# Stores of split weight tiles move from the sync engine's queue to GpSimd's

## The chip, the cores and the metric

The kernel runs on one core of a Trainium2 chip. The metric is the device time of one execution in microseconds (us). A core has a matrix engine (PE, with its weight loads PEld), a vector engine (DVE), a scalar engine (ACT), GpSimd (POOL) and a sync engine (SP). Each works through its own list of instructions in order; they wait for one another by semaphores. Transfers between device memory (HBM) and on-chip memory run on DMA engines and are started by an instruction in one engine's list, called here the issue. A transfer has landed when its semaphore says so.

## The reference

Causal attention over 4 x 12 heads of 448 x 64, then two feed-forward blocks over the 1792 x 768 tokens:

```python
x = softmax(mask(q @ k.T / 8)) @ v          # 4 x 12 heads, then joined to 1792 x 768
a = x @ w1;  b = x @ w2                     # 768 -> 1024
y = ((a * b) @ w3) @ w_out                  # 1024 -> 1024 -> 768
h = y @ w_in                                # 768 -> 2048
out = (h - np.tanh(h)) @ w_out2             # 2048 -> 768
```

All inputs are fp32, and the answer is wanted to fp32 accuracy.

## The kernel before

Every matrix product is made of three products of split numbers: each fp32 operand becomes a high part and a low part, and `gemms` (L411 to L413) adds high x low, low x high and high x high into one PSUM tile. The two weights w3 and w_out are multiplied with each other first (`product`). The tokens are worked in two halves of 896, each in two blocks of 384 and 512 columns.

Weights are split once, by `convert`. For each weight tile (a `Job`) the raw bits are loaded (`load`, L295, ring `raw` of two buffers), rescaled on ACT (`low`, L304), put together on DVE (`rounded`, L314, L317 and L321, ring `t` of two buffers), rounded to the high part (`high`, the copy of L267) and subtracted to give the low part (`rest`, the subtraction of L270 on POOL or DVE). The first half of the tokens uses some of these tiles on the spot. The split tiles are also stored to HBM (`store`, L327), because both halves need them, and read back later by `fetch` (L375). The 56 stored tiles are 16 of w1 and w2 (buffers `hl`, ring of three, to `sc12`), 16 of w_in (4 through the single buffer `cvi`, 12 through the two buffers `cvo`, to `sci`) and 24 of the last w_out (through the same two buffers `cvo`, to `sco`). A `cvo` tile is used by nothing else: its buffer is free for the next job but one when its store has landed.

The split of the last 24 tiles runs beside the products of the second half of the tokens: `bilinear` makes a and b, with two PSUM buffers (`r_mm`, L252). The tile of a is copied out by ACT or DVE (`keep`, L267), the tile of b is multiplied with it by DVE (`mult`, L801), and the product is split into the `g` tiles (L267 on ACT, then L270 on POOL). After it `project` runs with eight PSUM buffers.

The order of each engine's list is fixed when the program is built. The class `Plan` keeps a model clock for each engine and for the DMA queue and writes down the step that can start first. `store` asks the model for DMA time alone (`yield dma(...)`), and no time of the engine that issues it. So its instruction goes into the issuing engine's list at the place that the model clock of the DMA queue gives.

Of the kernel before, what the change touches and what calls it, by code (L numbers as in the profile page):

```python
# [19 lines left out]
F32 = mybir.dt.float32  # L20
# [177 lines left out]
def act(n, psum=False):  # L198
    return "ACT", (0.104 if psum else 0.147) + n / 1400
# [8 lines left out]
def dves(n):  # L208

    return "DVE", 0.068 + n / 960, True  # L210


def dve2(n):

    return "DVE", 0.068 + n / 1920, True


def pool(n):
    return "POOL", 0.00244 * n, True
# [11 lines left out]
def dma(size):  # L231
    return "DMA", max(0.5, size / 330e3)
# [3 lines left out]
def body(ctx: ExitStack, tc: tile.TileContext, qkd, vd, vd4, w12, w3t, wo, w_in, wo2, out):  # L236
    nc = tc.nc
    V, A, G, SP, PE = nc.vector, nc.scalar, nc.gpsimd, nc.sync, nc.tensor
# [27 lines left out]
    def copy(eng, out, in_):  # L266
        A.copy(out=out, in_=in_) if eng == "ACT" else V.tensor_copy(out=out, in_=in_)  # L267

    def sub(eng, out, in0, in1):
        (V if eng == "DVE" else G).tensor_tensor(out=out, in0=in0, in1=in1, op=ALU.subtract)  # L270
# [17 lines left out]
    def convert(jobs, r_raw, r_t):  # L288

        def load():  # L290
            for j in jobs:
                plan.rank(j.rank)
                j.raw = yield r_raw
                yield dma(P * j.n * 8)
                SP.dma_start(out=j.raw.t[:, :j.n].rearrange("p n t -> p (n t)"), in_=j.src.bitcast(U32))  # L295
                plan.set(j.loaded)

        def low():
            for j in jobs:
                plan.rank(j.rank)  # L300
                yield j.loaded
                u = j.raw.t[:, :j.n, 0]
                yield act(j.n + 130)
                A.activation(out=u, in_=u, func=AF.Copy, scale=2.0 ** -29)  # L304
                plan.set(j.low)

        def rounded():
            for j in jobs:
                plan.rank(j.rank)
                yield j.loaded  # L310
                j.t = yield r_t
                raw, t, n = j.raw.t, j.t.t[:, :j.n], j.n
                yield dve2(1.25 * n)
                V.tensor_scalar(out=t, in0=raw[:, :n, 1], scalar1=3, scalar2=0x3FFFFFF8,  # L314
                                op0=ALU.logical_shift_left, op1=ALU.bitwise_and)
                yield dves(n)
                V.scalar_tensor_tensor(out=t, in0=raw[:, :n, 1], scalar=0xC0000000, in1=t,  # L317
                                       op0=ALU.bitwise_and, op1=ALU.bitwise_or)
                yield j.low
                yield dves(1.1 * n)  # L320
                V.tensor_tensor(out=t, in0=t, in1=raw[:, :n, 0], op=ALU.add)  # L321
                plan.done(j.raw)
                plan.set(j.rounded)

        def store(j):
            yield dma(P * j.n * 8)
            SP.dma_start(out=j.scratch, in_=j.buf.t[:, :, :j.n].bitcast(F32))  # L327
            plan.done(j.buf)
            plan.set(j.stored)

        def high():
            for j in jobs:
                plan.rank(j.rank)
                yield j.rounded
                j.parts = yield from j.dest(j)
                copy((yield [act(j.n), dve2(j.n)]), j.parts[0], j.t.t[:, :j.n].bitcast(F32))
                plan.set(j.high)

        def rest():
            for j in jobs:  # L340
                plan.rank(j.rank)
                yield j.high
                hi, lo = j.parts
                sub((yield [pool(j.n), dves(j.n)]), lo, j.t.t[:, :j.n].bitcast(F32), hi.bitcast(F32))
                plan.done(j.t)
                if j.scratch is not None:
                    j.buf.users = 1 + j.used
                    plan.spawn(store(j), j.rank)
                plan.set(j.ready)

        for f in (load, low, rounded, high, rest):
            plan.spawn(f(), jobs[0].rank)
# [761 lines left out]
```

## Time and profile before

| what | us |
|---|---|
| median of 3 runs (lowest 1064.9, highest 1068.66) | 1067.23 |
| the profiled execution | 1062.6 |
| its span, first to last instruction | 1060.8 |
| PE busy in the span | 1036.4 |
| DVE busy | 643.3 |
| ACT busy | 619.4 |
| POOL busy | 242.5 |

The span is the profiled execution without the 1.8 us around it. A busy time is the sum over an engine's instructions; issuing a DMA or waiting is not counted as busy. An average over the span hides that stages differ; the stretch between 460 and 580 us is the one that the rows below look at most.

### The profile page before, as it was taken

Reading aid. Unit: us, or ns where it says so; the run is one execution under the profiler, and the core shown is the slowest. Engines: PE = TensorE matmul, PEld = TensorE weight load, DVE = VectorE, ACT = ScalarE, POOL = GpSimd, SP = SyncE. Lnnn points to the kernel's source line nnn. Section 1 sums busy time; section 2 is a strip of 40 time slices with the busy share of each in tenths; the row PEclk is TensorE's granted clock in tenths of the full one; section 3 lists DMA queues with packets and bytes.
Section 4 is the critical chain, followed back from the end, with each engine's and each line's share of the span. In section 5 each row is a group of like instructions: output and inputs, shape, how many; then the busy total and the mean of one; then the engine's idle time right before and its main releaser. Section 6 shows DMA issues by size and latency. Waiting matters only on the chain.

```text
span 1060.8 us, 19813 instructions
## 1 busy us (share of the span) xinstructions
PE 1036.4 (98%) x7680; PEld 899.3 (85%) x7680; DVE 643.3 (61%) x1316; ACT 619.4 (58%) x1353; POOL 242.5 (23%) x188
## 2 busy tenths in 40 slices
PE   5799999999999999999999999999999999999998
PEld 3577788778888989888998989899888988988987
DVE  7886556667665466656565377384756655474742
ACT  6997868788776243433432488573736556553620
POOL 3542131222223400124532022121111111121210
PEclk8999999999999999999999999999999999999999
DMA  7674449877764798999998333233333543233124
GB/s 265 205 215 161 121 149 315 298 255 253 251 223 159 295 366 301 347 323 319 354 326 300 142 118 119 90 129 109 109 110 117 167 140 115 92 120 117 44 87 155
DMA packets 72318, 209.03 MB, mean 197 GB/s; under 512 B 6113, under 2 KB 21473, under 8 KB 70689
## 3 DMA queue, kind: packets, MB, share of 16 engines
q1 hardware_dynamic: 72224, 207.77, 57.0%
q8 instruction: 60, 0.98, 0.4%
q14 instruction: 34, 0.27, 0.1%
HBM read 155.45 MB, written 52.30 MB: 196 GB/s over the span
## 4 chain that ended last, share of the span: by engine, by line
PE 91%; ACT 3%; DMA 2%; DVE 2%; issue 1%; POOL 0%; SPq 0%; ACTq 0%; DVEq 0%
PE mm L411 28%; PE mm L413 27%; PE mm L412 27%; PE pv L683 3%; PE sc L657 2%; PE att L541 1%; DMA raw<-w3t 1%; ACT p L501 1%; PE att L488 1%; PE att L513 1%; ACT pt L267 1%; ACT raw L304 1%; DVE p L459 1%; DMA qk<-qkd 1%; DVE t L321 0%
## 5 line engine op out<-in xcount | busy, mean ns | idle before, releaser
L411 PE MATMUL mm<-x,hl 128*128 128x384 f32 (+1 forms) x768 | 282.1, 367 | 0.0
L413 PE MATMUL mm<-x,hl 128*128 128x384 f32 (+1 forms) x768 | 278.8, 363 | 0.0
L412 PE MATMUL mm<-x,hl 128*128 128x384 f32 (+1 forms) x768 | 278.6, 363 | 0.0
L270 POOL TENSOR_TENSOR g<-g 128x384 fp32r<-128x384 f32 (+1 forms) x64 | 76.7, 1199 | 371.1 <-ACT g L267 371.1
L411 PEld LDWEIGHTS mm<-x,hl 128*128 128x128 f32 x768 | 144.1, 188 | 18.7 <-issue 2.0
L413 PEld LDWEIGHTS mm<-x,hl 128*128 128x128 f32 x768 | 144.1, 188 | 15.3
L412 PEld LDWEIGHTS mm<-x,hl 128*128 128x128 f32 x768 | 144.2, 188 | 14.7
L413 PE MATMUL mm<-g,w 128*128 128x384 f32 (+1 forms) x384 | 139.6, 364 | 0.0
L412 PE MATMUL mm<-g,w 128*128 128x384 f32 (+1 forms) x384 | 139.4, 363 | 0.0
L411 PE MATMUL mm<-g,w 128*128 128x384 f32 (+1 forms) x384 | 139.1, 362 | 0.0
L897 DVE SCALAR_TENSOR_TENSOR g<-r,g 128x512 f32<-128x512 f32 (+1 forms) x192 | 124.7, 659 | 20.4 <-ACT r L888 17.6
L888 ACT ACTIVATE r<-sq,cst 128x384 f32<-128x384 f32 (+1 forms) x192 | 123.6, 666 | 8.0 <-DVE g L897 8.0
L411 PE MATMUL mm<-g,hl 128*128 128x384 f32 (+1 forms) x320 | 116.3, 363 | 2.1 <-POOL g L270 2.1
L413 PE MATMUL mm<-g,hl 128*128 128x384 f32 (+1 forms) x320 | 113.0, 353 | 0.0
L412 PE MATMUL mm<-g,hl 128*128 128x384 f32 (+1 forms) x320 | 112.9, 353 | 0.0
L881 DVE SCALAR_TENSOR_TENSOR g<-sq,mm 128x384 f32<-128x384 f32 (+1 forms) x64 | 39.6, 619 | 109.2 <-ACT th L879 108.6
L314 DVE TENSOR_SCALAR t<-raw 128x512 uint32<-128x512 uint32 (+1 forms) x80 | 52.3, 654 | 69.6 <-DMA raw<-wo 39.1
L875 ACT ACTIVATE sq<-mm 128x384 f32<-128x384 f32 (+1 forms) x64 | 34.7, 543 | 92.5 <-PE mm L413 92.4
L304 ACT ACTIVATE raw<-raw 128x512 uint32<-128x512 uint32 (+1 forms) x80 | 63.9, 799 | 33.7 <-DMA raw<-wo 16.3
L270 POOL TENSOR_TENSOR hl<-t,hl 128x512 fp32r<-128x512 f32 (+1 forms) x32 | 52.1, 1635 | 134.0 <-ACT hl L267 99.1
L321 DVE CUSTOM_DVE_ANT_0 t<-raw,t 128x1024 uint16<-128x1024 uint16 (+1 forms) x80 | 75.1, 938 | 6.7 <-ACT raw L304 0.2
L412 PEld LDWEIGHTS mm<-g,w 128*128 128x128 f32 x384 | 72.1, 188 | 8.0
(81 smaller groups left out, 1599.0 us busy)
## 6 DMA issues: line engine op xcount, KB each, us to landing
hl<-sci SPq DMA_DIRECT2D x32, 768.0 KB, 4.6
w<-sco SPq DMA_DIRECT2D x48, 512.0 KB, 3.5
raw<-w SPq DMA_DIRECT2D x16, 768.0 KB, 5.7
sc<-hl SPq DMA_DIRECT2D x16, 768.0 KB, 4.4
raw<-w_in SPq DMA_DIRECT2D x16, 768.0 KB, 6.7
hl<-scp SPq DMA_DIRECT2D x12, 1024.0 KB, 6.5
hl<-sc SPq DMA_DIRECT2D x16, 768.0 KB, 7.0
raw<-wo SPq DMA_DIRECT2D x24, 512.0 KB, 6.7
```

What stands on the lines that cost most here:

```text
L270: (V if eng == "DVE" else G).tensor_tensor(out=out, in0=in0, in1=in1, op=ALU.subtract)
L304: A.activation(out=u, in_=u, func=AF.Copy, scale=2.0 ** -29)
L314: V.tensor_scalar(out=t, in0=raw[:, :n, 1], scalar1=3, scalar2=0x3FFFFFF8, op0=ALU.logical_shift_left, op1=ALU.bitwise_and)
L321: V.tensor_tensor(out=t, in0=t, in1=raw[:, :n, 0], op=ALU.add)
L411: PE.matmul(ps, wh, xl, start=k == 0, stop=False)
L412: PE.matmul(ps, wl, xh, start=False, stop=False)
L413: PE.matmul(ps, wh, xh, start=False, stop=k == last)
L683: PE.matmul(ps.t[e * D:(e + 1) * D, a, have[0] * 32:P], v.t[r, kb, e], x, start=kb == 0, stop=kb == block(a, 4 - 1))
L875: A.activation(out=sq, in_=h, func=AF.Square)
L881: V.scalar_tensor_tensor(out=g, in0=sq, scalar=LEAD, in1=h, op0=ALU.mult, op1=ALU.mult)
L888: A.activation(out=rk.t[:, :n], in_=sq, func=AF.Square, bias=cst[:, k:k + 1])
L897: V.scalar_tensor_tensor(out=g, in0=rk.t[:, :n], scalar=QUAD[k][1], in1=g, op0=ALU.add, op1=ALU.mult)
```

## The change

The store of a split tile is issued by GpSimd instead of the sync engine:

```diff
         def store(j):
             yield dma(P * j.n * 8)
-            SP.dma_start(out=j.scratch, in_=j.buf.t[:, :, :j.n].bitcast(F32))
+            G.dma_start(out=j.scratch, in_=j.buf.t[:, :, :j.n].bitcast(F32))
             plan.done(j.buf)
             plan.set(j.stored)
```

The planner's model is the same, so the lists of PE, DVE and ACT are the same row for row. The 56 stores leave SP's list and stand in POOL's, each at the place that the model clock gave it.

POOL's list at the first tiles of the last w_out, before. `cvo_5471`, `cvo_5536`, `cvo_5576` and `cvo_5628` are the buffers of tiles 0 to 3, `g` the split of the product a * b; a name such as DMAHW4 is the semaphore of a transfer that was started by SP, DMASW0 of one started by POOL.

```order
L270 TENSOR_TENSOR g_5150<-asb_5442,g_5150 128x512 [waits Activation_49]
L270 TENSOR_TENSOR cvo_5471<-t_5436,cvo_5471 128x512 [waits DMAHW4_49,DMAHW5_49,DMAHW3_49,DMAHW7_49,DMAHW1_49,Activation_49]
L270 TENSOR_TENSOR g_5150<-asb_5411,g_5150 128x384 [waits Activation_49]
L270 TENSOR_TENSOR cvo_5536<-t_5485,cvo_5536 128x512 [waits DMAHW4_49,DMAHW1_49,DMAHW6_49,DMAHW0_49,Activation_49]
L270 TENSOR_TENSOR cvo_5576<-t_5542,cvo_5576 128x512 [waits DMAHW4_49,Activation_49]
L270 TENSOR_TENSOR g_5150<-asb_5557,g_5150 128x512 [waits Activation_49]
L270 TENSOR_TENSOR g_5150<-asb_5525,g_5150 128x384 [waits Activation_49]
L270 TENSOR_TENSOR cvo_5628<-t_5582,cvo_5628 128x512 [waits DMAHW7_49,Activation_49]
```

The same place in POOL's list now:

```order
L270 TENSOR_TENSOR g_5150<-asb_5442,g_5150 128x512 [waits Activation_49]
L327 DMA sci_15_123<-cvo_5430 128x1536 [waits DMASW7_49]
L270 TENSOR_TENSOR cvo_5471<-t_5436,cvo_5471 128x512 [waits DMASW4_49,DMASW2_49,DMASW6_49,DMASW0_49,Activation_49]
L270 TENSOR_TENSOR g_5150<-asb_5411,g_5150 128x384 [waits Activation_49]
L270 TENSOR_TENSOR cvo_5536<-t_5485,cvo_5536 128x512 [waits DMASW5_49,DMASW3_49,DMASW7_49,DMASW1_49,Activation_49]
L327 DMA sco_0_124<-cvo_5471 256x1x512 [waits Pool_49]
L270 TENSOR_TENSOR cvo_5576<-t_5542,cvo_5576 128x512 [waits DMASW0_49,Activation_49]
L327 DMA sco_1_125<-cvo_5536 256x1x512 [waits Pool_49]
L270 TENSOR_TENSOR g_5150<-asb_5557,g_5150 128x512 [waits Activation_49]
L270 TENSOR_TENSOR g_5150<-asb_5525,g_5150 128x384 [waits Activation_49]
L327 DMA sco_2_126<-cvo_5576 256x1x512 [waits Pool_49]
L270 TENSOR_TENSOR cvo_5628<-t_5582,cvo_5628 128x512 [waits DMASW1_49,Activation_49]
```

The store of tile 0 stands behind the subtraction of tile 1, that of tile 1 behind the subtraction of tile 2, that of tile 2 behind two subtractions of `g`.

POOL's list at tiles 9 to 14 now (`cvo_5854`, `cvo_5908`, `cvo_5942`, `cvo_5977`, `cvo_6025`, `cvo_6068`):

```order
L327 DMA sco_9_133<-cvo_5854 256x1x512 [waits Pool_49]
L270 TENSOR_TENSOR cvo_5908<-t_5853,cvo_5908 128x512 [waits DMASW0_49,Activation_49]
L270 TENSOR_TENSOR cvo_5942<-t_5907,cvo_5942 128x512 [waits DMASW1_49,Activation_49]
L327 DMA sco_10_134<-cvo_5908 256x1x512 [waits Pool_49]
L270 TENSOR_TENSOR g_5151<-asb_5926,g_5151 128x512 [waits Activation_49]
L327 DMA sco_11_135<-cvo_5942 256x1x512 [waits Pool_49]
L270 TENSOR_TENSOR cvo_5977<-t_5941,cvo_5977 128x512 [waits DMASW2_49,Activation_49]
L270 TENSOR_TENSOR g_5151<-asb_5894,g_5151 128x384 [waits Activation_49]
L270 TENSOR_TENSOR cvo_6025<-t_5976,cvo_6025 128x512 [waits DMASW3_49,Activation_49]
L327 DMA sco_12_136<-cvo_5977 256x1x512 [waits Pool_49]
L270 TENSOR_TENSOR cvo_6068<-t_6031,cvo_6068 128x512 [waits DMASW4_49,Activation_49]
```

Before, the subtractions stand there in the same order and nothing between them; the stores of tiles 10 and 12 now stand behind the subtraction of the next tile.

SP's list at the first of these tiles, before:

```order
L327 DMA sci_15_123<-cvo_5430 128x1536
L375 DMA hl_5496<-sc12_8_94 128x2x768
L295 DMA raw_5484<-wo2 128x1024
L327 DMA sco_0_124<-cvo_5471 256x1x512
L375 DMA hl_5555<-sc12_9_95 128x2x768
L295 DMA raw_5541<-wo2 128x1024
L327 DMA sco_1_125<-cvo_5536 256x1x512
L295 DMA raw_5581<-wo2 128x1024
```

And now:

```order
L375 DMA hl_5496<-sc12_8_94 128x2x768
L295 DMA raw_5484<-wo2 128x1024
L375 DMA hl_5555<-sc12_9_95 128x2x768
L295 DMA raw_5541<-wo2 128x1024
L295 DMA raw_5581<-wo2 128x1024
```

SP keeps its loads and fetches in their order, and no longer waits for POOL's subtraction between them.

## Rows read from the trace of the kernel before

**Rows 1.** The page: busy time (share of span) and count; the chain's shares by engine.
```profile
PE 1036.4 (98%) x7680; PEld 899.3 (85%) x7680; DVE 643.3 (61%) x1316; ACT 619.4 (58%) x1353; POOL 242.5 (23%) x188
...
PE 91%; ACT 3%; DMA 2%; DVE 2%; issue 1%; POOL 0%; SPq 0%; ACTq 0%; DVEq 0%
```

**Rows 2.** Stretches: length, then busy us and count by engine, clock, DMA share, GB/s.
```profile
466.00:536.00 70.00, 70.00 (x348) 62.53 (x347) 42.40 (x54) 28.91 (x50) 33.21 (x25) 1.00 0.95 334
...
700.00:800.00 100.00, 100.00 (x501) 90.27 (x500) 60.44 (x101) 49.22 (x91) 17.12 (x14) 1.00 0.34 111
```

**Rows 3.** Waits of PE, 160 to 600 us: total us, times, longest.
```profile
PE pv L683 <- issue: 1.0, 2, 0.7
```

**Rows 4.** Waits of ACT and DVE from 460 to 580 us, in the same columns.
```profile
DVE t L314 <- DMA raw<-wo: 38.3, 18, 4.8
...
ACT cvo L267 <- DMA sco<-cvo: 15.3, 6, 5.4
```

**Rows 5.** Waits of SP's queue over the whole span, in the same columns.
```profile
SPq L327 <- POOL cvo L270: 39.7, 21, 3.3
```

**Rows 6.** DMA issues: count, KB of one, median us from issue to landing.
```profile
w<-sco SPq DMA_DIRECT2D x48, 512.0 KB, 3.5
...
sc<-hl SPq DMA_DIRECT2D x16, 768.0 KB, 4.4
...
sco<-cvo SPq DMA_DIRECT2D x24, 512.0 KB, 5.4
...
sci<-cvo SPq DMA_DIRECT2D x12, 768.0 KB, 8.0
...
sci<-cvi SPq DMA_DIRECT2D x4, 768.0 KB, 3.2
```

**Rows 7.** POOL by time: start us, length us, instruction, [idle before, what ended it].
```profile
434.51 3.57 POOL L270 TENSOR_TENSOR g<-asb,g 128x512 fp32r<-128x512 f32 x2 [68.01 <-ACT g L267]
...
463.96 1.29 POOL L270 TENSOR_TENSOR g<-asb,g 128x512 fp32r<-128x512 f32 x1 [12.43 <-ACT g L267]
466.94 1.30 POOL L270 TENSOR_TENSOR cvo<-t,cvo 128x512 fp32r<-128x512 f32 x1 [1.69 <-DMA sci<-cvo]
...
471.51 1.29 POOL L270 TENSOR_TENSOR cvo<-t,cvo 128x512 fp32r<-128x512 f32 x1 [2.11 <-ACT cvo L267]
...
511.08 1.21 POOL L270 TENSOR_TENSOR g<-asb,g 128x384 fp32r<-128x384 f32 x1
...
533.29 1.33 POOL L270 TENSOR_TENSOR cvo<-t,cvo 128x512 fp32r<-128x512 f32 x1 [3.85 <-ACT cvo L267]
...
575.75 1.29 POOL L270 TENSOR_TENSOR cvo<-t,cvo 128x512 fp32r<-128x512 f32 x1 [3.01 <-ACT cvo L267]
```

**Rows 8.** SP's queue by time, in the same columns: two stores.
```profile
460.77 0.33 SPq L327 DMA_DIRECT2D sci<-cvo  x1
...
472.83 0.55 SPq L327 DMA_DIRECT2D sco<-cvo  x1
```

**Rows 9.** ACT by time, in the same columns.
```profile
466.24 0.62 ACT L267 CAST cvo<-t 128x512 fp32r<-128x512 f32 x1 [2.36 <-DMA sci<-cvo]
...
470.81 0.62 ACT L267 CAST cvo<-t 128x512 fp32r<-128x512 f32 x1 [2.50 <-DVE t L321]
471.34 0.58 ACT L267 COPY asb<-mm 128x512 f32<-128x512 f32 x1
```

**Rows 10.** DVE by time, in the same columns.
```profile
467.21 1.32 DVE L314 TENSOR_SCALAR t<-raw 128x512 uint32<-128x512 uint32 x1 [2.95 <-DMA raw<-wo]
...
479.37 0.43 DVE L314 TENSOR_SCALAR t<-raw 128x512 uint32<-128x512 uint32 x1 [3.66 <-DMA raw<-wo]
...
480.44 0.55 DVE L801 TENSOR_TENSOR asb<-mm,asb 128x384 f32<-128x384 f32 x1
```

**Rows 11.** PE by time, in the same columns: the first matmul of a tile.
```profile
481.09 0.45 PE L411 MATMUL mm<-x,hl 128*128 128x512 f32 x1
```

## The prediction

> **What bounds the kernel now.** I read the page first. PE is busy for 98% of the span and makes up 91% of the chain that ended last [rows 1], so a change counts only where it makes PE wait or spares it a wait. Next the stretches: from 466 to 536 us, where many of the moved stores lie, PE is busy for 70.00 of 70.00 us and runs 348 matmuls, 4.97 in a us; from 700 to 800 us, where no tile is split or stored, it runs 501, or 5.01 in a us [rows 2]. So the stage with the stores runs as fast as the stage without them. The list of waits says the same: between 160 and 600 us, which holds all 56 stores, PE waited for 1.0 us in all, and for nothing that the trace names [rows 3]. There is nothing here for the change to win back. What there is to lose is told by the engines that empty PE's two PSUM buffers. DVE's multiplication at 480.44 ends at 480.99, and PE starts the next tile in that buffer at 481.09 [rows 10, 11]: DVE had 0.1 us to spare. DVE and ACT are that late because in their fixed lists they first wait for the splitting of the weights: DVE 38.3 us for raw tiles, ACT 15.3 us, six times, for a stored `cvo` buffer to come free [rows 4]. So the question is whether the moved stores make those waits longer.
>
> **What the change removes.** SP loses 56 issues, and with them its wait for POOL's subtraction, 39.7 us in 21 waits [rows 5]; those 21 stores left in the moment in which they were ready. The loads behind them may go out sooner. Worth: at most the 1.0 us that PE waits, and I take 0.
>
> **What it adds on POOL.** 56 issues. What one costs on POOL the trace of before doesn't show. SP takes 0.33 to 0.55 us for one [rows 8]; a POOL subtraction of 512 columns takes 1.29 us [rows 7]. I take SP's 0.55, which is already part of the landing times below, since nothing is computed; 1.29 would add 0.74 to each. As work it fits: POOL is busy 33.21 of 70 us [rows 2], and the 15 stores there would add 8 to 20. A price below nothing is excluded: the instruction is new on POOL.
>
> **What it moves, where it costs nothing.** The 16 `hl` stores land 4.4 us after their issue [rows 6]. Their ring has three buffers, and a tile stays in its buffer anyway until PE has used it for two blocks of 18 matmuls, 2 x 18 x 0.20 = 7.2 us (0.20 is 70/348). That hides the store; without this cover it would cost one landing at each turn of the ring. The four `cvi` stores land in 3.2 us [rows 6]; on POOL they follow their own subtraction directly, as on SP, so only a dearer issue could cost, 4 x 0.74 = 3 us at most. Of the 12 `sci` stores from `cvo` the first seven find POOL empty: it had waited 68.01 us when it began the subtraction at 434.51 [rows 7]. They leave when their tile is ready, as before.
>
> **What it moves, where it costs.** From 434 us on POOL's list holds the splits of the product, and stores stand behind them. The last `sci` store left SP at 460.77 [rows 8]; on POOL it stands behind the subtraction of 463.96, which ends at 465.25 [rows 7]. With the median landing of 8.0 [rows 6] it is through at 473.25. Tile 1 of the last w_out needs that buffer, and its copy on ACT began at 470.81 [rows 9]: 2.4 us late.
>
> Then the 24 `sco` stores. There are two buffers, so tile n+2 can be rounded only when the store of tile n has landed. Before, a store left as soon as its own subtraction had ended: that of tile 1 ends at 472.80 and SP issues at 472.83 [rows 7, 8]. Now the lists show the store of tile 0 behind the subtraction of tile 1, that of 1 behind 2, 4 behind 5, 7 behind 8, 10 behind 11 and 12 behind 13. Where store n waits for subtraction n+1, and subtraction n+2 for the landing of store n, the two buffers no longer overlap: one follows the other. One such link costs a landing of 5.4 us [rows 6] plus the copy on ACT and the subtraction, from 466.24 to 468.24, 2.0 us [rows 7, 9]: 7.4 us. The longest path from subtraction 1 to subtraction 14 goes through the tiles 1, 2, 3, 5, 6, 8, 9, 11, 12, 13, 14. Nine of its steps are such links (3 to 5, 6 to 8 and 9 to 11 are the ordinary loop over two tiles, with one subtraction of `g`, 1.21 us [rows 7], ahead of store 9); 12 to 13 is a plain step at the mean distance, 61.8/13 = 4.75. That makes 9 x 7.4 + 1.2 + 4.75 = 72.6 us. Before, subtraction 1 ends at 472.80 and subtraction 14 at 534.62 [rows 7], 61.8 us. So the splitting falls 10.8 us behind, with the 2.4 from above 13.2.
>
> **What of it reaches PE.** ACT and DVE are bound to the order of their lists, so a late `cvo` copy holds up the copy out of PSUM right behind it (470.81, then 471.34 [rows 9]). With two PSUM buffers an evacuation can be late by at most one tile, 18 x 0.20 = 3.6 us, less its own 0.58; at 480.44 nothing is left of that. I take half of 3.0 as spare: 13.2 - 1.5 = 11.7, about 12 us that PE waits.
>
> From tile 14 on (until 577.04, the end of the last subtraction [rows 7]) the same links cost again: six of them and two plain steps, 6 x 7.4 + 2 x 4.75 = 53.9 us instead of 42.4. But by then `project` runs with eight PSUM buffers, six more than before, each a tile of 24 matmuls: 6 x 24 x 0.20 = 29 us of cover. I cost it at nothing; without the cover it is 11.5 us more.
>
> Sum: the profiled execution took 1062.6 us, its span 1060.8; with 12 us the span becomes 1073 and the execution 1075. The median of the runs, 1067.2, lies 4.6 above the profiled execution, so I forecast 1067.2 + 12 = **1079 us**.
>
> The bounds are those of the landing. The lowest is 3.5 us, the fetch of the same 512 KB at a time when little else is moved, the highest 8.0, the `sci` stores in the crowded stretch [rows 6]. A link is then 5.5 or 10.0. I take 5.4 since it is the same transfer at the same place, with the DMA engines 95% busy [rows 2].
>
> The Trainium skill (DMA: Bandwidth & Descriptors, section Latency and other measured facts) gives about 1 us to the first byte for a transfer started by GpSimd and about 0.6 for one started by SP. By it each link would be 0.4 longer and the time about 1083; no run so far shows it.
>
> **Rivals.**
>
> *No change, 1067.* A store of 768 KB lands in 3.2 us where little else is queued and in 8.0 behind SP's loads [rows 6]. In a queue of its own it may no longer stand behind them. At 3.5 us the path is 9 x 5.5 + 6 = 55.5, under 61.8, and the last `sci` store is through at 465.25 + 3.5 = 468.8, ahead of 470.81: nothing is late. It decides from a landing of 4.2, a link of 6.2. Against it: the DMA engines are 95% busy there [rows 2], whoever starts the transfer. The skill (same page, section Issuing engines are not separate DMA queues) says that transfers from all issuers end on the same DMA engines, so that another issuer saves only the time of the issue. By that rule this rival loses chance; the rows can't show it.
>
> *Much slower, about 1102.* POOL and DVE get in each other's way: an instruction of L314 took 1.32 us at 467.21, when POOL's subtraction of 466.94 was running, and 0.43 at 479.37 [rows 7, 10]. If an issue on POOL is held up in that way, the landing goes to the upper bound of 8.0: 9 x 10.0 + 6 - 61.8 = 34.2, with 2.4 and less 1.5 some 35 us. For it: DVE is busy 42.40 of 70 us [rows 2]. Against it: few of its instructions are of that kind. The skill (SBUF — State Buffer, section SBUF: two separate sides) says that GpSimd's cores write the descriptors of such a transfer and can't while DVE holds the port that they share. That is a rule against this change; that the two exclude each other, L314 agrees.
>
> *Faster, about 1066.* SP's loads come sooner and shorten DVE's 38.3 us. PE waits 1.0 us there, so no more than that can be won.
>
> That the change doesn't do what it says can be left out: the lists show all 56 stores on POOL.
>
> **How the numbers follow.** A measurement of this kernel can tell 0.3%, 3.2 us, from no change. I give the forecast (4 to 20 us slower) 0.53, much slower 0.24, no change 0.20, faster 0.03. So slower by over 0.3% has 0.77, within 0.3% 0.20, faster by over 0.3% 0.03. The range leaves out about a tenth at each end: it begins at 1066, inside the case of no change, and ends at 1098, 31 us slower, a link of 9.5.
>
> **What would show it.** Right: POOL issues the `sco` stores after the next tile's subtraction; from subtraction 1 to 14 some 72 us pass instead of 62; ACT's wait for `sco` landings rises from 15.3 to well over 30 us; PE waits for ACT or DVE between 470 and 545 us, some 12 us in all, and not elsewhere. Wrong: PE's waits stay at 1 us (landing under 4.2, or more spare than I took), or they go on beyond 545 (the eight buffers don't cover), or they come where `hl` and `cvi` are stored.

## The result and the profile after

The changed kernel takes 1082.67 us (median of 4 runs, 1077.15 to 1084.13), beside 1067.88 for the kernel before (4 runs, 1064.9 to 1068.66): a ratio of 1.0129, interval 1.0096 to 1.0163. A second measurement, among the experiments below, gives 1.0163 (1.0141 to 1.0185). So it is 14 to 17 us slower; 12 were forecast. Its profiled execution is the fastest of its runs: 1077.15 us, span 1075.4.

The page of the changed kernel, the lines that answer to [rows 1]: busy time and count, and the chain by engine.

```profile
PE 1037.9 (97%) x7680; PEld 898.7 (84%) x7680; DVE 652.7 (61%) x1316; ACT 615.4 (57%) x1353; POOL 275.2 (26%) x244
...
PE 75%; DMA 11%; ACT 6%; DVE 3%; POOL 2%; issue 2%; SPq 0%; ACTq 0%; DVEq 0%; POOLq 0%
```

PE's busy time is the same as before to 1.5 us; its share of the chain falls from 91% to 75%, and DMA's rises from 2% to 11%. The stretch from 466 to 536 us of the changed kernel, in the columns of [rows 2], says where:

```profile
466.00:536.00 70.00, 63.74 (x311) 55.67 (x310) 42.31 (x46) 20.14 (x38) 33.80 (x34) 1.00 0.87 293
```

PE is busy for 63.74 us instead of 70.00 there. From 700 to 800 us, where nothing is stored, it is busy all the time, as before. The waits of the changed kernel, PE's from 160 to 600 us first ([rows 3]), then those of ACT and DVE from 460 to 580 us ([rows 4]): total us, times, longest.

```profile
PE mm L411 <- ACT asb L267: 5.2, 3, 2.2
PE mm L411 <- DVE asb L801: 3.2, 3, 1.4
PE mm L411 <- POOL g L270: 2.8, 1, 2.8
...
ACT cvo L267 <- DMA sco<-cvo: 53.8, 12, 7.2
...
DVE t L314 <- DMA raw<-wo: 12.6, 8, 4.2
```

PE now waits 11.2 us for the engines that empty its PSUM buffers and for one subtraction of `g`. ACT's wait for a stored `cvo` buffer has gone from 15.3 to 53.8 us. DVE's for raw tiles has fallen from 38.3 to 12.6. That is not because SP, which no longer waits for POOL, loads earlier: in the kernel before, eight of the twelve loads between 462 and 520 us already left within 0.04 us of the moment in which DVE freed their buffer. DVE and SP of the kernel before:

```profile
480.91 0.68 DVE L321 CUSTOM_DVE_ANT_0 t<-raw,t 128x1024 uint16<-128x1024 uint16 x1
481.62 0.33 SPq L295 DMA_DIRECT2D raw<-wo  x1
```

DVE waits less for raw tiles and waits for ACT instead, 29.5 us from 460 to 580 us for the rescaling of L304. That stands in ACT's list behind the `cvo` copy for which ACT waits.

The reason for ACT's wait stands in POOL's list. POOL of the changed kernel by time, then ACT, in the columns of [rows 7]:

```profile
466.55 1.30 POOL L270 TENSOR_TENSOR cvo<-t,cvo 128x512 fp32r<-128x512 f32 x1
...
474.49 1.30 POOL L270 TENSOR_TENSOR cvo<-t,cvo 128x512 fp32r<-128x512 f32 x1 [5.67 <-ACT cvo L267]
475.73 0.68 POOL L327 DMA_DIRECT2D sco<-cvo  x1
481.46 1.29 POOL L270 TENSOR_TENSOR cvo<-t,cvo 128x512 fp32r<-128x512 f32 x1 [5.05 <-ACT cvo L267]
482.70 0.71 POOL L327 DMA_DIRECT2D sco<-cvo  x1
...
473.79 0.62 ACT L267 CAST cvo<-t 128x512 fp32r<-128x512 f32 x1 [5.57 <-DMA sci<-cvo]
474.32 0.58 ACT L267 COPY asb<-mm 128x512 f32<-128x512 f32 x1
480.75 0.62 ACT L267 CAST cvo<-t 128x512 fp32r<-128x512 f32 x1 [5.29 <-DMA sco<-cvo]
```

The subtraction of 474.49 is tile 1's, and the store of 475.73 is tile 0's: ready since 467.85, when subtraction 0 (466.55) ended, it was issued 7.9 us later. ACT waits for its landing until 480.75, then comes subtraction 2 at 481.46, and only behind that, at 482.70, the store of tile 1. That is the serial link. The copy out of PSUM behind the waiting ACT (474.32) is the one that PE needs.

The DMA issues of the changed kernel, in the columns of [rows 6]:

```profile
sc<-hl POOLq DMA_DIRECT2D x16, 768.0 KB, 4.5
...
sco<-cvo POOLq DMA_DIRECT2D x24, 512.0 KB, 4.7
...
sci<-cvo POOLq DMA_DIRECT2D x12, 768.0 KB, 7.3
...
sci<-cvi POOLq DMA_DIRECT2D x4, 768.0 KB, 3.8
```

In the median a store from POOL lands about as fast as one from SP (4.4, 5.4, 8.0 and 3.2 before).

### The profile page after: what moved, and what is told of

The parts are those of the page before. It is cut to its first block, busy times and chain, and to the rows that moved or that the text cites. A ratio compares the mean times of both kernels' runs of the same rounds, so it can differ in the third digit from the quotient of the medians.

```text
span 1075.4 us, 19797 instructions
## 1 busy us (share of the span) xinstructions
PE 1037.9 (97%) x7680; PEld 898.7 (84%) x7680; DVE 652.7 (61%) x1316; ACT 615.4 (57%) x1353; POOL 275.2 (26%) x244
## 4 chain that ended last, share of the span: by engine, by line
PE 75%; DMA 11%; ACT 6%; DVE 3%; POOL 2%; issue 2%; SPq 0%; ACTq 0%; DVEq 0%; POOLq 0%
PE mm L411 23%; PE mm L413 22%; PE mm L412 22%; DMA sco<-cvo 4%; PE pv L683 3%; PE sc L657 2%; DMA sci<-cvo 2%; ACT p L501 2%; DMA raw<-w 2%; PE att L488 1%; DMA raw<-w3t 1%; POOL cvo L270 1%; PE att L541 1%; PE att L513 1%; ACT raw L304 1%
## 5 line engine op out<-in xcount | busy, mean ns | idle before, releaser
L321 DVE CUSTOM_DVE_ANT_0 t<-raw,t 128x1024 uint16<-128x1024 uint16 (+1 forms) x80 | 80.2, 1002 | 41.3 <-ACT raw L304 36.6
L314 DVE TENSOR_SCALAR t<-raw 128x512 uint32<-128x512 uint32 (+1 forms) x80 | 56.1, 701 | 48.2 <-POOL hl L270 13.8
L267 ACT CAST cvo<-t 128x512 fp32r<-128x512 f32 (+1 forms) x36 | 24.9, 692 | 104.8 <-DMA sco<-cvo 64.0
```

## The experiments

Theory A: the loss is the place of the store in POOL's in-order list. Theory B: a store that POOL starts is itself dearer. The table has the results beside three readings of each trace: PE's busy time in the 150 us from 450 to 600, its mean granted clock there (1.00 is the upper level), and the time from the end of subtraction 1 to that of subtraction 14, all of the one profiled execution. Times and ratios are against the kernel before on the same chip.

| kernel | median, us | ratio, interval | PE of 150 us | clock there | 1 to 14, us |
|---|---|---|---|---|---|
| before | 1067.88 | | 150.00 | 1.00 | 61.8 |
| changed | 1082.67 | 1.0129 (1.0096, 1.0163) | 138.73 | 1.00 | 74.9 |
| changed, again | 1085.56 | 1.0163 (1.0141, 1.0185) | 137.91 | 0.97 | 77.1 |
| all 56 on POOL, at once | 1068.30 | 1.0004 (0.9985, 1.0023) | 148.32 | 1.00 | 66.7 |
| only 24 `sco` on POOL | 1084.58 | 1.0159 (1.0129, 1.0188) | 137.75 | 0.98 | 81.0 |
| the other 32 on POOL | 1068.27 | 1.0012 (0.9994, 1.0029) | 149.35 | 1.00 | 60.2 |
| `sco` 0 to 13 on POOL | 1084.34 | 1.0143 (1.0113, 1.0174) | 137.31 | 0.97 | 81.7 |
| `sco` 14 to 23 on POOL | 1067.00 | 1.0014 (0.9995, 1.0032) | 149.88 | 1.00 | 63.2 |
| all on SP, 11 late | 1073.46 | 1.0059 (1.0036, 1.0082) | 144.84 | 0.99 | 69.2 |
| all on SP, 17 late | 1075.50 | 1.0081 (1.0064, 1.0098) | 140.99 | 1.00 | 73.4 |
| the same, again | 1075.51 | 1.0070 (1.0043, 1.0098) | 142.95 | 0.99 | 70.7 |
| 17 late, POOL sends 2 KB | 1087.34 | 1.0187 (1.0163, 1.0211) | 135.23 | 0.98 | 80.9 |
| 17 late, POOL clears a tile | 1080.58 | 1.0101 (1.0071, 1.0132) | 140.41 | 0.97 | 75.1 |

### All 56 stores on POOL, each behind its own subtraction

```diff
 def store(j):
     yield dma(P * j.n * 8)
-    G.dma_start(out=j.scratch, in_=j.buf.t[:, :, :j.n].bitcast(F32))
 def rest():
     ...
         if j.scratch is not None:
+            G.dma_start(out=j.scratch, in_=j.buf.t[:, :, :j.n].bitcast(F32))
             j.buf.users = 1 + j.used
```

> All 56 stores stay on GpSimd, but each is issued directly behind the subtraction that made its tile; the lists of the other four engines are those of the changed kernel. Theory A (the loss is the place of the store in GpSimd's list: behind the next tile's subtraction): the serial links of 5.8 to 8.3 us in the stretch from 460 us go, subtraction 1 to 14 takes 62 to 65 us instead of 74.9, TensorE waits under 4 us there, time 1067 to 1071. Theory B (a store that GpSimd starts is itself dearer: a longer issue, a slower transfer, a contended port): the landings and the waits stay, time 1078 or more. Between the two, 1072 to 1077, both have a share.

Measured: 1068.3, no difference to the kernel before. PE's waits from 160 to 600 us and POOL by time in this run:

```profile
PE mm L411 <- POOL g L270: 1.7, 1, 1.7
PE pv L683 <- issue: 1.5, 1, 1.5
```
```profile
471.91 1.29 POOL L270 TENSOR_TENSOR cvo<-t,cvo 128x512 fp32r<-128x512 f32 x1 [1.29 <-ACT cvo L267]
473.65 0.71 POOL L346 DMA_DIRECT2D sco<-cvo  x1 [0.45 <-POOL cvo L270]
```

Tile 1's store (473.65) is issued 0.45 us behind its own subtraction. POOL issues as many stores as in the changed kernel, at 0.69 us each for `sco` in the mean, and they land in 6.3 us, slower than the 4.7 above; the loss is gone all the same. The place is what the loss needs. Only the 66.7 us lie over the 62 to 65 that were expected: the path is 4.9 us longer than before, and PE loses 1.7 us of the 150.

### Which stores: 24 `sco`, or the other 32

```diff
-G.dma_start(out=j.scratch, ...)
+(G if j in jobs_out else SP).dma_start(out=j.scratch, ...)
```

> Only the 24 stores of the output projection's tiles (sco) are issued by GpSimd, the other 32 by SyncE as before. Theory A: nearly the whole loss, 9 to 14 us over the kernel before (1076 to 1082), short by the 2 to 3 us of the entry, where the last sci store is again on time. Theory B: the loss goes with the number of stores moved, 24 of 56, so about 6 us (1074).

> The complement: the other 32 stores (sci, cvi, hl) on GpSimd, the 24 of sco on SyncE. Theory A: 0 to 3 us over the kernel before (1067 to 1071), since only the last sci store stands before a tile that is late. Theory B (by number of stores, 32 of 56): about 8 us (1076).

The second kernel has `not in` for `in`. The 24 `sco` stores alone cost 1.59%, as much as all 56 and more than the 9 to 14 us expected; the other 32 cost 0.12%, with an interval that includes nothing. By number of stores it would have been 6 and 8 us. The gap to all 56, the 2 to 3 us of the entry, did not show: with the last `sci` store on SP, tile 1 is in time, but subtraction 14 still ends 85.6 us after subtraction 0 (81.0 + 4.6), against 82.8 (74.9 + 7.9) in the changed kernel. The path alone differs by 7 us between kernels with the same late stores (74.9 to 81.7), which is more than the entry.

### Which tiles: the first 14, or the last 10

The same line, with `jobs_out[:14]` and `jobs_out[14:]`.

> Only the first 14 sco stores (tiles 0 to 13) are on GpSimd, all others on SyncE. By the same claim: nearly the whole loss, 10 to 17 us over the kernel before (1078 to 1085), all of TensorE's waits between 470 and 560 us. Rival (every late tile costs): 14/24 of it, 8 to 10 us (1076 to 1078).

> Only the last ten sco stores (tiles 14 to 23) are on GpSimd, all others on SyncE. The prediction's claim that lateness from tile 14 on is covered by the eight PSUM buffers: 0 to 2 us over the kernel before (1067 to 1070), though the subtractions 14 to 23 take 46 to 54 us instead of 42.4. Rival (every late tile costs): 10/24 of the loss of the 24, 5 to 7 us (1073 to 1075).

The stretches 466 to 536 and 536 to 606 us, first of the kernel with tiles 14 to 23 on POOL, then of the one with tiles 0 to 13, in the columns of [rows 2]:

```profile
466.00:536.00 70.00, 69.88 (x350) 62.83 (x349) 40.69 (x53) 27.72 (x48) 30.77 (x23) 1.00 0.95 330
536.00:606.00 70.00, 70.00 (x352) 63.22 (x351) 32.93 (x45) 20.40 (x36) 23.70 (x23) 1.00 0.82 289
```
```profile
466.00:536.00 70.00, 63.89 (x309) 56.26 (x308) 37.16 (x43) 20.57 (x38) 30.73 (x29) 0.98 0.81 282
536.00:606.00 70.00, 63.43 (x298) 55.90 (x297) 36.69 (x46) 22.22 (x40) 24.27 (x21) 0.95 0.81 285
```

Ten late stores from tile 14 on cost PE 0.12 us of the 140, though subtraction 14 to 23 takes 49.2 us instead of 42.4. The first fourteen cost the whole loss. The cover of the PSUM buffers can be seen in the kernel with tiles 14 to 23 on POOL; ACT, DVE and PE by time:

```profile
582.88 0.62 ACT L267 CAST cvo<-t 128x512 fp32r<-128x512 f32 x1 [7.96 <-DMA sco<-cvo]
...
586.63 0.69 DVE L270 TENSOR_TENSOR x<-mm,x 128x512 fp32r<-128x512 f32 x1 [1.22 <-ACT x L828]
...
583.76 0.33 PE L411 MATMUL mm<-g,hl 128*128 128x384 f32 x1
```

ACT waits 8.0 us for a landing, and behind it the PSUM tile that PE finished at 579.7 is emptied only at 587.3. PE has begun the next tile at 579.6 and the one after at 583.8, without a wait. With two buffers that last tile would have needed the one that was still full, 3.6 us longer.

### Late stores without GpSimd

SP issues every store, but where it stood behind a later tile's subtraction in the changed kernel it first sends 4 bytes of that tile:

```diff
-G.dma_start(out=j.scratch, ...)
+if subbed and subbed[-1] is not j:
+    SP.dma_start(out=late_[len(subbed)], in_=subbed[-1].buf.t[0:1, 1, 0:1].bitcast(F32))
+SP.dma_start(out=j.scratch, ...)
```

> GpSimd issues nothing; SyncE issues all stores, but 11 of the sco stores are held until the subtraction of a later tile is done (the one behind which GpSimd's store stood in the changed kernel), by a 4-byte transfer that reads that tile and is queued ahead of the store; these 11 small transfers are the only thing added. Theory A (place alone, whichever engine issues): 6 to 14 us over the kernel before, with SyncE issuing (1073 to 1082), ScalarE again waiting for sco landings for well over 30 us. Theory B (GpSimd's own part): 0 to 3 us over (1067 to 1071).

It holds 11 stores. The next kernel holds the five `sco` stores behind subtractions of `g` as well, and the last `sci`: `lastsub[-1]`, the output of POOL's last subtraction of any kind, in the place of `subbed[-1]`.

> As the run in which SyncE issued late, but now every store of sco, and the last of sci, is held on SyncE until the GpSimd subtraction behind which it stood in the changed kernel is done, those on tiles g too: 17 held stores instead of 11, each by a 4-byte transfer queued ahead of it (these 17 are the only thing added). Theory A (place alone): the remaining difference comes back, 10 to 16 us over the kernel before (1078 to 1084). Theory B (what was left in that run is GpSimd's own: its longer issue, its subtractions pushed back by the issues in between): it stays at 5 to 8 us over (1073 to 1076).

SP of this second kernel by time, and PE's waits from 160 to 600 us:

```profile
473.25 0.24 SPq L272 DMA_DIRECT2D late<-cvo  x1
473.58 0.56 SPq L340 DMA_DIRECT2D sco<-cvo  x1
```
```profile
PE mm L425 <- DVE asb L815: 4.8, 2, 3.2
PE mm L425 <- issue: 2.5, 1, 2.5
PE mm L425 <- ACT asb L275: 1.7, 1, 1.7
```

Lateness costs without GpSimd: 0.59% with 11 late stores, 0.81% with 17, and 0.70% when repeated. That is about half of the changed kernel's loss, with 11 late stores at the lower end of what theory A expected, with 17 below it. Theory A's other sign failed: ACT waits 25.3 us for `sco` landings with 11 late stores and 22.6 with 17, not well over 30. These kernels are no pure measure of the place either: a held store holds SP's loads behind it, and DVE waits for raw tiles longer than before. From 460 to 580 us in the kernel with 17:

```profile
DVE t L324 <- DMA raw<-wo: 47.5, 17, 5.5
...
ACT cvo L275 <- DMA sco<-cvo: 22.6, 8, 4.0
```

(12.6 and 53.8 in the changed kernel.) The path is nearly as long, 73.4 and 70.7 us of subtractions against 74.9 and 77.1, though GpSimd starts none of the transfers; but a part of it is now the wait for raw tiles. So late stores lengthen the path whichever engine starts them. That the links alone would make it as long is not shown.

### What is the other half?

Four runs, two of them repeats, for the difference between the 7 to 9 us here and the 14 to 17 of the changed kernel.

```diff
 SP.dma_start(out=j.scratch, ...)
+if j in jobs_out:
+    G.dma_start(out=extra_[len(mark)], in_=cst)
```

> As the run in which SyncE issued all 17 late stores (1.0081 of the kernel before), and in addition GpSimd issues, at the 24 places of the sco stores in its list, a transfer of its own of 2 KB (128 rows of a constant tile to an unused place) that nothing waits for. Theory B (the rest of the loss is GpSimd's time: its issues push its subtractions back and stretch VectorE's work): the time rises to that of the changed kernel, 11 to 17 us over the kernel before (1078 to 1085), and VectorE's conversion rows grow. Theory C (the rest is only what a longer wait does behind it, as a fall of TensorE's granted clock, and differs from run to run): it stays at 7 to 10 us over (1074 to 1077) or nearly, with VectorE's rows as short.

> The changed kernel once more on the same chip, for the comparison: 12 to 16 us over the kernel before (1079 to 1083). By theory C its runs differ by the granted clock of the stretch from 470 to 560 us: where the profile has waits of over 2 us there, a stretch with the clock below 1 follows some of them; by theory B the clock is no part of it.

The time rose to 1.87%, above the changed kernel's, but not in the way of theory B: VectorE's rows stayed short. Its third conversion from 465 to 600 us, with mean ns behind the busy us, in the changed kernel and in this one:

```profile
L321 DVE CUSTOM_DVE_ANT_0 t<-raw,t 128x1024 uint16<-128x1024 uint16 x23 | 24.1, 1046 | 37.5 <-ACT raw L304 36.6
```
```profile
L331 DVE CUSTOM_DVE_ANT_0 t<-raw,t 128x1024 uint16<-128x1024 uint16 x22 | 16.2, 737 | 2.7
```

Instead the transfers look dearer. With the 24 small ones the DMA engines, 86% busy from 466 to 536 us, moved 262 GB/s; without them 281 at 80%. The two kernels in the columns of [rows 2]:

```profile
466.00:536.00 70.00, 60.58 (x285) 52.44 (x284) 31.02 (x43) 21.67 (x38) 28.79 (x29) 0.98 0.86 262
```
```profile
466.00:536.00 70.00, 63.47 (x315) 56.33 (x314) 33.88 (x45) 24.07 (x42) 26.41 (x21) 1.00 0.80 281
```

So this run seems to have brought in a cost of its own and decides nothing between B and C. The changed kernel, measured again, came out at 1.63%, above what was expected, with the clock lowered behind two of its waits, as theory C has it (last section). The next has POOL occupied without a transfer:

```diff
+if j in jobs_out:
+    for _ in range(5):
+        G.memset(idle_, 0.0)
```

> As the run in which SyncE issued all 17 late stores, and in addition GpSimd clears a small tile of its own five times (about 0.6 us together) at the 24 places of the sco stores in its list; no transfer is added to GpSimd. Theory B (the rest of the changed kernel's loss is that GpSimd is occupied there): the time rises from 8.6 us to 12 to 17 us over the kernel before (1079 to 1085). Rival (it is not the occupied time): it stays at 7 to 10 us over (1075 to 1078), and the rest has to do with the transfers that GpSimd starts or with the granted clock.

> The run in which SyncE issued all 17 late stores, once more beside it on the same chip: 7 to 10 us over the kernel before (1075 to 1078) if the first measurement holds; 12 us or more would say that the difference to the changed kernel was one of chips or runs and that the place of the stores is the whole loss.

1.0101 (1.0071 to 1.0132) beside 1.0070 (1.0043 to 1.0098): the occupied time may add some 3 us to the 7.5. The median, 1080.58, lies in the range of theory B, but the intervals overlap, and the ratio falls short of 1.0163. In its trace PE idles for 9.6 of the 150 us, hardly more than without the occupation (9.0 and 7.1); what is new is the clock, 0.97.

The table places most of the other half, though from single executions. In the four profiles with the first 14 `sco` stores late on POOL (changed, again, only `sco`, `sco` 0 to 13) PE idles for 11.3 to 12.7 of the 150 us, 12.1 in the mean, and by the mean clock another 3.0 us are lost. In the two with 17 late on SP it is 8.0 and 0.8. So an estimate of the half is 4 us of longer waits and 2 us of lowered clock; the rest is not placed.

Why PE waits longer stays open. What is shown: it exists only together with the late place, since GpSimd's stores cost nothing where they go out at once. A candidate, not proven, is that in the changed kernel the lateness shows on ACT (53.8 us of waiting for landings), which is also the engine that empties PSUM; VectorE then waits for ACT's part of the conversion (36.6 us above) and not for raw tiles. VectorE's longer row alone is not it: with all stores at once that row is as long, 1074 ns in the mean, without loss.

## Why the prediction held, step by step

**PE is the bound and nothing can be won**: right. SP's relief is worth nothing; the fall of DVE's wait from 38.3 to 12.6 us has another reason (see the result).

**The price of an issue on POOL**: under-sized. 0.55 was taken, with 1.29 as the upper end; the stores of 512 KB took 0.73 us in the mean, the `sci` ones from `cvo` 0.54. POOL by line in the changed kernel (mean ns behind the busy us):

```profile
L327 POOL DMA_DIRECT2D sco<-cvo x24 | 17.2, 732 | 1.7 <-POOL cvo L270 1.2 <-DMA sco<-cvo 0.4
```

As a price it is nothing: with all stores at once the time is that of before.

**`hl`, `cvi` and the first `sci` stores cost nothing**: right. The 32 stores cost 0.12%, within what a measurement can't tell from nothing.

**The entry, 2.4 us**: seen, as 3.0. ACT's copy of tile 1 came at 473.79 instead of 470.81. What it is worth as a term of the sum can't be told: without it the loss is as large, beside a path that varies by more.

**The serial links**: right in mechanism and nearly in size. From subtraction 1 to 14 the sum said 72.6 us; the first and the second profile of the changed kernel have 74.9 and 77.1, and two other kernels with the same late stores 81.0 and 81.7. The parts were off in both directions. In the first profile the six links measured singly (1 to 2, 2 to 3, 5 to 6, 8 to 9, 11 to 12, 13 to 14) take 7.0, 6.0, 5.8, 6.3, 7.6 and 8.3 us, a mean of 6.8 where 7.4 was taken; the ordinary loops 3 to 5, 6 to 8 and 9 to 11 take 9.8, 9.7 and 11.5 where 7.4, 7.4 and 8.6 were taken; the plain step 12 to 13 takes 2.9 where 4.75 was taken. The loops were under-sized by their landing. The store of 489.24, tile 3's, left directly behind its subtraction, and ACT waited for it until 496.50, 7.3 us; for that of 475.73 until 480.75, 5.0 us. POOL and ACT of the changed kernel:

```profile
489.24 0.68 POOL L327 DMA_DIRECT2D sco<-cvo  x1 [0.45 <-DMA sco<-cvo]
...
496.50 0.62 ACT L267 CAST cvo<-t 128x512 fp32r<-128x512 f32 x1 [5.41 <-DMA sco<-cvo]
```

Why some stores land later than others the runs don't say. The median landing, the term on which the range hung, was 4.7 and 5.8 us in the two profiles; 5.4 was taken. The Trainium skill (DMA: Bandwidth & Descriptors, section Issuing engines are not separate DMA queues) says that starting transfers on several engines saves only the time that the issues take. These landings agree. The Trainium skill's larger time to the first byte for a transfer from GpSimd (same page, section Latency and other measured facts), from which the prediction estimated 0.4 us more per link, can't be told from their spread.

**What reaches PE, about 12 us in 470 to 545**: 8.4 us in that stretch of the first profile, in six waits for ACT or DVE, as was said. With a seventh, 2.8 us for POOL's subtraction of `g` that ends at 553.6, it is 11.2. That this is so close to 12 is in part luck. The splitting fell further behind than the sum had it, 13.1 us on the path and 3.0 at the entry instead of 10.8 and 2.4, and less of it came through: 8.4 of 16.1 us, where all but 1.5 was to. So the spare was under-sized, and a longer path and an unforeseen wait made up for it. POOL at the time of the seventh wait:

```profile
549.38 1.28 POOL L270 TENSOR_TENSOR cvo<-t,cvo 128x512 fp32r<-128x512 f32 x1 [6.34 <-ACT cvo L267]
...
551.24 2.30 POOL L270 TENSOR_TENSOR g<-asb,g 128x512 fp32r<-128x512 f32 x2
```

The last `g` tiles stand behind subtraction 14, and PE's next stage needs them. "Not elsewhere" was wrong by this one wait: the prediction looked at what empties PSUM and not at what else POOL's list holds up. From then on the eight buffers cover, as said; the subtractions 14 to 23 take 46.8 and 48.8 us in the two profiles, where 53.9 was reckoned.

**The total**: 1079 said, 1082.7 and 1085.6 measured, 4 and 7 us more. The first profile, 1077.15, lies close to 1062.6 + 12, but it is the fastest of nine executions; the others lie 4 to 10 us above it. The kernel before scatters as much, from 1062.6 to 1072.7, and for that the sum had its 4.6 us. What no step had is the lowered clock behind the new waits: 5.1 us in the second profile, none in the first (last section). How much of the 4 and 7 us it is the runs don't separate.

**The rivals.** "No change" needed a landing under 4.2 us, and the median landing was 4.7 and more; it is also what the kernel with stores at once gives, by another way. "Much slower" needed issues held up until landings reach 8.0; in the median they didn't. That VectorE and POOL hold each other up is seen, though (the row at 499.08 below): it falls on VectorE. The Trainium skill (SBUF — State Buffer, section SBUF: two separate sides) says that GpSimd can't write a transfer's descriptors while VectorE holds the port that they share. No row here ties a late landing to that.

## What to carry to other kernels

An instruction that is moved to an in-order queue gets a new place in that queue, and the place can cost more than the instruction: ask what stands ahead of it there, and whether a buffer that the thing ahead needs is freed by it. With two buffers, a store that waits for the next tile's work turns an overlap into a chain; the same stores, issued directly behind the work that made them, cost nothing on either engine. Lateness on a helper engine was paid here where the busy engine had two PSUM buffers, and was free where it had eight.

## What had not been expected of the hardware

**The clock falls behind a wait.** PE's windows in the second profile of the changed kernel, with the granted clock third from the end, and below them the same places in the first:

```profile
488.00:492.00 4.00, 1.70 (x8) 1.08 (x6) 2.79 (x2) 0.97 (x2) 2.71 (x4) 1.00 1.03 292
492.00:498.00 6.00, 5.38 (x17) 4.26 (x18) 2.35 (x3) 2.08 (x5) 2.50 (x3) 0.72 0.98 347
...
556.00:566.00 10.00, 6.70 (x18) 5.50 (x19) 7.03 (x8) 2.14 (x5) 6.00 (x7) 0.66 0.59 177
```
```profile
492.00:498.00 6.00, 6.00 (x35) 5.88 (x34) 2.39 (x5) 1.50 (x3) 0.80 (x1) 1.00 0.67 248
...
556.00:566.00 10.00, 10.00 (x46) 8.40 (x46) 7.00 (x8) 3.76 (x7) 5.18 (x6) 1.00 0.81 292
```

PE waited 2.9 us until 492.6 and 3.8 us until 559.3, and behind both the granted clock was at 1.2 instead of 2.4 GHz for a part of the window: 17 matmuls where the first profile has 35, 18 where it has 46. A part of that is the wait itself, 0.6 and 3.3 us of these windows; the lost clock is 6 x 0.28 + 10 x 0.34 = 5.1 us. The first profile has a wait of 2.8 us that ends at 553.6 and no lowered clock behind it. The other profiles agree: between 464 and 612 us the clock is lowered only behind a wait of PE, the shortest of 1.8 us (only `sco` on POOL), and other waits of up to 3.2 us (17 late on SP) leave it as it is. So a wait can cost more than its length, in some executions and not in others.

Not every lowered clock comes from the change. The first profile's mean clock over the span is 0.998, its time 1077; the other eight runs of this kernel have 0.987 to 0.994 and take 1081 to 1087. But from 40 to 60 us, long before the first store, the clock is 1.00 in the first profile and 0.76 in the second, another 4.8 us, and the kernel before ranges from 0.988 to 0.998 too.

**VectorE is held through two subtractions of POOL.** DVE and POOL of the changed kernel by time:

```profile
483.22 2.76 DVE L314 TENSOR_SCALAR t<-raw 128x512 uint32<-128x512 uint32 x1
499.08 3.46 DVE L314 TENSOR_SCALAR t<-raw 128x512 uint32<-128x512 uint32 x1
...
483.32 2.38 POOL L270 TENSOR_TENSOR g<-asb,g 128x512 fp32r<-128x512 f32 x2
...
499.17 1.38 POOL L270 TENSOR_TENSOR g<-asb,g 128x512 fp32r<-128x512 f32 x1
500.40 0.80 POOL L327 DMA_DIRECT2D sco<-cvo  x1
501.02 1.22 POOL L270 TENSOR_TENSOR g<-asb,g 128x384 fp32r<-128x384 f32 x1
```

An instruction that takes 0.43 us alone and 1.32 beside a subtraction [rows 10] took 3.46 us where POOL ran two subtractions with a store between them and no gap, and 2.76 us where two subtractions followed each other without a store. So the stores are not shown to be the reason.
